# Attention with two heads in halves of the array's rows, four chunks of 112 tokens a unit

## The chip, the core and the metric

The kernel runs on one core of a Trainium2 chip. The metric is the device time of one execution in microseconds (us), taken as the median of several. The engines that matter here are TensorE (PE in the profile, with its weight loads shown apart as PEld), VectorE (DVE), ScalarE (ACT), GpSimd (POOL), and SyncE (SP), which issues most of the DMAs. Matmuls accumulate in PSUM, which has eight banks of 2 KB a partition; a bank holds 512 float32 columns. A matmul uses as many rows of the 128x128 array as its contraction has elements, and as many columns as its weights have.

## The reference

Attention over 8 batches, 12 heads, 448 tokens and a head size of 64, with RMS-normed queries and keys; then a top-1 mixture of experts over the 3584 tokens of 768 features.

```python
q_n, k_n = (rmsnorm(q, g_q), rmsnorm(k, g_k))
scores = scale * np.matmul(q_n, k_n.transpose(0, 1, 3, 2))
scores = scores - np.max(scores, axis=-1, keepdims=True)
attn = np.exp(scores)
attn = attn / (np.sum(attn, axis=-1, keepdims=True) + 1e-09)
attn_out = np.matmul(attn, v)
x = attn_out.transpose(0, 2, 1, 3).reshape(3584, 768)
logits = x @ w_gate + modality_bias[modality_id]
e_idx = np.argmax(logits, axis=1)           # one of 8 experts
gate_w = softmax(logits)[np.arange(3584), e_idx]
for e in range(8):
    mask = e_idx == e
    h = np.maximum(x[mask] @ w1[e], 0.0)    # 768 to 1024
    out[mask] = gate_w[mask, None] * (h @ w2[e])
```

## The kernel before, in words

**Order.** The program is a list of instructions for each engine, in an order that is written out by hand. The attention is a loop over steps n; a table PLAN says at which step each piece of a unit is issued, relative to the unit's own steps. Small operations of the routing wait in a list, and a function pump releases a few of them at each step. Waits between engines follow from the tiles: an instruction that writes a tile waits for the instructions that still read it. Such a dependence goes by the tile, and one allocated twice from a pool of two buffers gives two tiles that don't depend on each other.

**Units and steps.** A unit is one batch and one pair of heads, so there are 48. In the kernel before it has 2 x 448 = 896 keys, cut into seven tiles of 128; tile 3 straddles the two heads. Each unit has seven steps.

**Preparing q and k.** `norm` scales q and k by their root mean squares on POOL; the squares are taken on ACT and summed on DVE (`sumsq`). `tr` (L750) transposes four blocks of 112 tokens of both heads on PE into one PSUM bank, 64 features of head 0 above 64 of head 1. The result is split in two parts of lower precision so that products come out accurate: ACT copies a high part (`a0`), DVE subtracts it to get the low part. Then ACT makes two more copies of half the partitions each (`a1`, `a2`, with a 64x64 copy each for q), and SP issues moves by DMA (`move`, L763), so that the operands stand twice, or stacked high above low. In a unit there are eight such moves of 112 KB.

**Scores.** `sa` (L827, and L822 for tile 3) computes a first product, queries by keys, of 128 rows, one matmul a step into a bank of the pool ps_a (two buffers). DVE takes the maxima of its rows (TENSOR_REDUCE, 128x448). `mt` (L838) transposes the unit's maxima, and a DMA puts them as a 65th row under the low part of q. `st` (L855) computes the scores again, transposed and accurate, with two matmuls a step (128 rows, then 65 rows with the maxima subtracted; four for tile 3) into a bank of ps_s (two buffers). ACT takes the exponential into p.

**Behind the scores.** `av` (L894) multiplies p with v, head 0 into the upper and head 1 into the lower half of the array's columns. These are full float32, and the profile counts two records for each matmul. The eight matmuls of a unit are issued in three visits, in its steps 1, 4 and 6, one unit later. `csum` adds the tiles of p on POOL and DVE for the sums of rows; `sums` and `gates` (L909, L916) compute sums and routing logits; `xt` (L951) turns the output to token rows.

**MoE.** The second part of the program takes the tokens in slots of 256, 14 of them fixed. A slot transposes its tokens in three groups (`xtr`, L464 on; the name of its PSUM tile is px, from ps_a), splits each result in high (ACT) and low (DVE), and runs `mm1` (ph, L485, from ps_s, 18 matmuls for each half of four tiles, evacuated by ACT and DVE) and `mm2` (py, L515). The three transpose groups for the next slot stand within the `mm2` of the present one, at places 9, 11 and 13.

## Time and profile before

| what | value |
|---|---|
| runs | 1123.1, 1125.59, 1126.49 us; median 1125.59 |
| profiled execution | 1126.66 us; its span 1124.8 us |
| first scores matmul (st) starts | 42.1 us |
| last st, then first ph of the MoE | 576.0, then 577.8 us |
| PE busy share of the span | 95% |
| DVE, ACT, POOL busy shares | 77%, 73%, 59% |

The span is cut at 42.1, 577.8 and 662 us: until 42.1 the first unit is prepared, until 577.8 the steps of the attention run, until 662 the first MoE work overlaps the last of the routing, and from there on the MoE runs steadily. A view by windows gives for each stretch the busy time of each engine, with the number of instructions in brackets. A timeline gives one instruction, or several alike, per row: the start, the time, the engine, the line, and the result with its operands. Successive matmuls overlap in their records, so their spacing is read from the starts and not from the durations.

### The profile page before, as it was taken

The page shows a single profiled execution, that of the slowest core. Times are in us where ns is not written, and L with a number is a line of the kernel's source. Part 1 is how long each engine was busy: PE and PEld are TensorE (multiplying, and loading weights), DVE is VectorE, ACT ScalarE, POOL GpSimd, SP SyncE. Part 2 cuts the span into 40 slices and gives each one's busy share as a digit, 9 for nine tenths or more (in the row PEclk, how much of TensorE's full clock was granted, in tenths as well). Part 3 has the DMA queues.
Part 4 walks back from the last instruction along what each step waited for, and adds up shares of the span by engine and source line. Part 5 has one row for each costly group of instructions (what it writes and reads, how often), then busy time and mean ns, then how long its engine had stood idle before and what let it go on. Part 6 is the DMA issues. An engine that isn't in the chain of part 4 may idle for free.

```text
span 1124.8 us, 19920 instructions
## 1 busy us (share of the span) xinstructions
PE 1074.1 (95%) x6678; PEld 837.5 (74%) x6678; DVE 863.4 (77%) x1604; ACT 821.5 (73%) x1545; POOL 659.5 (59%) x658
## 2 busy tenths in 40 slices
PE   7899999999999999998999999999999999999993
PEld 6655555555555555554569989999999999999991
DVE  4677788888889877899699977667777677776770
ACT  5678888878778787876677577667876678766870
POOL 4477677778777688787865474354234432445440
PEclk7999999999999999999999999999999999999997
DMA  6656676677666777665833202111170111111360
GB/s 169 150 137 163 147 180 167 158 172 172 154 169 147 172 161 182 146 145 111 239 124 92 48 29 66 29 58 57 43 267 29 57 58 43 33 40 57 100 207 8
DMA packets 127969, 131.79 MB, mean 117 GB/s; under 512 B 68891, under 2 KB 122607, under 8 KB 126320
## 3 DMA queue, kind: packets, MB, share of 16 engines
q1 hardware_dynamic: 110212, 88.58, 33.5%
q0 software_dynamic: 17616, 41.80, 11.8%
q8 instruction: 57, 0.93, 0.4%
q14 instruction: 56, 0.46, 0.1%
q10 hardware_dynamic: 28, 0.01, 0.0%
HBM read 148.74 MB, written 22.38 MB: 152 GB/s over the span
## 4 chain that ended last, share of the span: by engine, by line
PE 75%; DVE 11%; DMA 7%; ACT 2%; issue 2%; POOL 1%; SPq 1%; ACTq 0%; DVEq 0%; POOLq 0%
PE ph L485 18%; PE py L515 16%; PE av L894 12%; PE st L855 12%; PE sa L827 5%; DMA lt<-l_d,tb_li 4%; PE tr L750 3%; DVE w1w L52 2%; DVE at_hlw L52 2%; PE xt L951 2%; PE sm L909 2%; PE px L468 2%; DMA w1w<-xw 1%; DVE xw L52 1%; DVE w2lw L52 1%
## 5 line engine op out<-in xcount | busy, mean ns | idle before, releaser
L485 PE MATMUL ph<-xw,w1w 128*128 128x256 f32 x2016 | 247.6, 285 | 3.0 <-DVE hlw L52 2.3
L485 PEld LDWEIGHTS ph<-xw,w1w 128*128 128x128 f32 x2016 | 245.3, 193 | 5.0 <-DVE hlw L52 2.5
L52 DVE TENSOR_REDUCE at_hlw<-sa 128x1 f32<-128x448 f32 x336 | 206.6, 617 | 44.4 <-PE sa L827 25.5
L52 DVE TENSOR_TENSOR w1w<-r,w1w 128x256 fp32r<-128x256 f32 x360 | 221.4, 672 | 13.3 <-ACT w1w L52 13.3
L52 ACT CAST w1w<-r 128x256 fp32r<-128x256 f32 x360 | 225.3, 732 | 0.5 <-DVE tb_t L53 0.4
L855 PE MATMUL st<-w1w 128*128 128x448 f32 (+1 forms) x480 | 175.5, 415 | 1.6 <-ACT r2w L52 1.6
L52 ACT ACTIVATE r2w<-st 128x448 f32<-128x448 f32 x168 | 90.9, 543 | 49.7 <-PE st L855 42.0
L52 ACT ACTIVATE hhw<-ph 128x512 fp32r<-128x512 f32 x56 | 33.5, 598 | 124.5 <-PE ph L485 124.5
L827 PE MATMUL sa<-w1w 128*128 128x448 f32 (+1 forms) x288 | 110.9, 386 | 14.1 <-DVE at_hlw L52 7.1
L855 PEld LDWEIGHTS st<-w1w 128*128 128x128 f32 (+1 forms) x480 | 84.8, 190 | 44.2 <-ACT r2w L52 21.8
L52 POOL TENSOR_TENSOR r2w<-r2w 128x448 f32<-128x448 f32 (+1 forms) x72 | 82.9, 1151 | 57.6 <-DVE r2w L52 18.5
L515 PE MATMUL py<-w2lw,hhw 128*128 128x384 f32 x448 | 114.0, 335 | 0.0
L52 ACT ACTIVATE at_w2lw<-st 128x448 f32<-128x448 f32 x168 | 90.9, 543 | 23.3 <-PE st L855 17.3
L52 ACT CAST w1w<-xw 64x448 fp32r<-64x448 f32 x188 | 105.3, 561 | 2.0
L855 PE MATMUL st<-w1w,w2ha 65*128 65x448 f32 x288 | 100.7, 370 | 1.8 <-DMA w1w<-xw 1.7
L52 POOL TENSOR_TENSOR xrw<-r,at_hlw 112x512 f32<-112x512 f32 x94 | 96.9, 1050 | 1.0 <-PE tr L750 0.7
L52 POOL DMA_INDIRECT out_dram<-yw,lb_oi x22 | 25.3, 1152 | 122.2 <-ACT yw L52 112.3
L515 PEld LDWEIGHTS py<-w2lw,hhw 128*128 128x128 f32 x448 | 80.9, 188 | 0.0
L52 DVE SCALAR_TENSOR_TENSOR hlw<-ph,hhw 128x512 fp32r<-128x512 f32 x56 | 38.7, 690 | 53.4 <-ACT hhw L52 53.4
L827 PEld LDWEIGHTS sa<-w1w 128*128 128x128 f32 (+1 forms) x288 | 55.3, 192 | 27.4 <-DVE at_hlw L52 13.0
L52 POOL TENSOR_TENSOR r2w<-r2w,at_w2lw 64x448 f32<-64x448 f32 (+1 forms) x48 | 55.3, 1152 | 30.3 <-DVE r2w L52 11.3
L52 POOL DMA_INDIRECT xrw<-x_d,lb_x2i x24 | 30.3, 1261 | 67.0 <-DMA xrw<-x_d,lt 63.4
(296 smaller groups left out, 2284.9 us busy)
## 6 DMA issues: line engine op xcount, KB each, us to landing
w1w<-xw SPq DMA_DIRECT2D x312, 112.0 KB
r<-in_q_dram SPq DMA_DIRECT2D x48, 224.0 KB
r<-in_k_dram SPq DMA_DIRECT2D x48, 224.0 KB
...
```

The costliest lines, as they stand in the source:

```text
L52: return fn(*a, **kw)
L468: PE.transpose(ps[:, i, 128 * t : 128 * t + 128], xr[t][:, 2 * g + i], idn)
L485: PE.matmul(ps[:, i], lhsT=lt_, rhs=rt_[:, c], start=n == 0, stop=n == 17)
L515: PE.matmul(ps[n][:, :384], lhsT=lt_[:, j, 128 * t : 128 * t + 128], rhs=rt_[:, 384 * n : 384 * n + 384], start=j == 0 and m == 0, stop=j ...
L750: PE.transpose(sp[:, c], src[:, c], idn[:CP, :CP])
L827: PE.matmul(ps[:, :S], lhsT=t["qq"][r, h, a : a + 128], rhs=t["kk"][h][r], start=True, stop=True)
L855: PE.matmul(ps[:, :S], lhsT=l, rhs=t["qq"][:, h] if first else t["ql"][:, h], start=first and (j != 3 or h == 0), stop=not first and (j != ...
L894: PE.matmul(t["av"][64 * h : 64 * h + 64, :S], lhsT=vv[r, u % 3, j], rhs=t["p"][r, j], start=c == 0, stop=c == 3)
L909: PE.matmul(R[g][32 * i : 32 * i + 32, :S], lhsT=sel[:, m], rhs=T[u + i // 2]["cs"][:, i % 2], start=m == 0, stop=False, tile_position=(0, ...
L951: PE.transpose(ps[:CP, 128 * c : 128 * c + 128], T[u]["xt"][:, c * CP : (c + 1) * CP], idn)
```

## The change

The chunk of keys and queries becomes 112 tokens of both heads (CP), and a unit four steps. Operands stay as the transposes leave them, with head 0 in partitions 0 to 63 (LO) and head 1 in 64 to 127 (HI). A new function `both_heads` issues for each pair of operands two matmuls of 64 rows, one on each half of the array's rows, into the two banks of one PSUM tile. The first product has one such pair a chunk, the accurate scores have four: high by high, low by high, high by low, and a pair that subtracts the maxima (ones in one row of each half, times a row `mr` of maxima). So a unit has 40 such matmuls in place of 23.

The two pools have one buffer of two banks each now. Their tiles, `pa` and `pb`, are allocated once and used for the whole program; the MoE's px, ph and the like take the two banks of pa or pb in turn through `bank`. One maximum and one exponential cover a chunk of both heads. The copies a1 and a2 and all eight moves a unit are gone; the maxima go through two small DMAs, and v is loaded by one DMA a unit in place of four. The low parts and high copies are issued in the step of their transposes, behind the exponential and the maximum. The four av pieces have a step each, behind the transposes of the step. PLAN has new numbers throughout, for steps of which there are four a unit; the loop starts at step -14 of these, before at -22 of the others.

```diff
-NJ = 7
+NJ = 4
-PLAN = {'rtj': 6, ..., 'av': (1, 1, 4, 6), ..., 'sa': 14, 'mt': 6, 'tk': 21, 'tq': 18, ..., 'start': -22, ...}
+PLAN = {'rtj': 1, ..., 'av': (0, 1, 2, 3), ..., 'sa': 7, 'mt': 3, 'tk': 9, 'tq': 10, ..., 'start': -14, ...}
...
-    ps_a = ctx.enter_context(tc.tile_pool(name="ps_a", bufs=2, space=PSUM))
-    ps_s = ctx.enter_context(tc.tile_pool(name="ps_s", bufs=2, space=PSUM))
+    ps_a = ctx.enter_context(tc.tile_pool(name="ps_a", bufs=1, space=PSUM))
+    ps_s = ctx.enter_context(tc.tile_pool(name="ps_s", bufs=1, space=PSUM))
...
+    pa = ps_a.tile([128, 2, 512], F32, tag="a", name="pa")
+    pb = ps_s.tile([128, 2, 512], F32, tag="s", name="pb")
+    turns = [0, 0]
+
+    def bank(w):
+        turns[w] ^= 1
+        return (pa, pb)[w][:, turns[w]]
...
     def xtr(s, xr, g):
-        ps = ps_a.tile([128, 2, TB], F32, tag="a", name=f"px{s}_{g}")
+        ps = bank(0).rearrange("p (i t) -> p i t", i=2)
...
     def mm1_open(s, jj):
-        return ps_s.tile([128, 2, TB], F32, tag="s", name=f"ph{s}_{jj}")
+        return bank(1).rearrange("p (i t) -> p i t", i=2)
...
+            SY.dma_start(t["v"][:CP, u % 3].rearrange("p h c d -> p h (c d)"),
+                         v[b, h0 : h0 + 2].rearrange("h (p c) d -> p h (c d)", p=CP))
...
-            h_, l_ = hi_b[u % 2][g], lo_b[g]
+            h_, l_ = t[nm] = qk_b[u % 4][2 * g : 2 * g + 2]
...
+        def both_heads(ps, c, *operands):
+            for n, (l, r) in enumerate(operands):
+                for h, rows in enumerate((LO, HI)):
+                    PE.matmul(ps[:CP, h, :S], lhsT=l[rows] if l is mone else l[rows, CP * c : CP * c + CP],
+                              rhs=r[rows],
+                              start=n == 0, stop=n == len(operands) - 1)
...
+            both_heads(pa, c, (t["q"][0], t["k"][0]))
 
             def dve():
-                V.tensor_reduce(out=t["mx"][:, j : j + 1], in_=ps[:, :S], op=ALU.max,
-                                axis=AX.X, negate=True)
+                V.tensor_reduce(out=t["mx"][:, :, c], in_=pa[:CP, :, :S], op=ALU.max, axis=AX.X, negate=True)
...
+                for h in range(2):
+                    SY.dma_start(t["mr"][64 * h : 64 * h + 1].bitcast(F32),
+                                 ms[NCH * h : NCH * h + NCH].bitcast(F32))
...
+            (qh, ql), (kh, kl) = t["q"], t["k"]
+            both_heads(pb, c, (kh, qh), (kl, qh), (kh, ql), (mone, t["mr"]))
 
             def act():
-                A.activation(out=t["p"][:, j], in_=ps[:, :S], func=AF.Exp)
+                A.activation(out=t["p"][:CP, c], in_=pb[:CP, :, :S], func=AF.Exp)
...
+            for h in range(2):
+                o = (c2_b if c < NCH - 1 else t["cs"])[:CP, h]
+                (V if c == 1 and h in CSV else G).tensor_tensor(
+                    out=o, in0=p[:CP, 0, h] if c == 1 else c2_b[:CP, h], in1=p[:CP, c, h], op=ALU.add)
...
-                j, r = (3, (LO, HI)[h]) if c == 3 else (4 * h + c, slice(0, 128))
-                PE.matmul(t["av"][64 * h : 64 * h + 64, :S], lhsT=vv[r, u % 3, j],
-                          rhs=t["p"][r, j], start=c == 0, stop=c == 3)
+                PE.matmul(t["av"][64 * h : 64 * h + 64, :S], lhsT=vv[:CP, u % 3, h, c],
+                          rhs=t["p"][:CP, c, h], start=c == 0, stop=c == NCH - 1)
```

**PE in the attention.** The first steps of a unit in the middle of the program stand on PE like this before (a row is an instruction with its line, result, operands and shape, and the semaphores that it waits for, each named after the engine or the DMA queue that raises it):

```order
L855 MATMUL st_0_2884<-w1w 128x448 [waits Activation_49]
L855 MATMUL st_0_2884<-w1w 128x448 [waits DMAHW7_49,DMAHW6_49,DMAHW2_49]
L827 MATMUL sa_0_2887<-w1w 128x448 [waits DMAHW3_49,DMAHW0_49,DVE_49]
L750 MATMUL tr_1_2889<-idn,xrw 128x112 [waits PE_49,Pool_49]
L750 MATMUL tr_1_2889<-idn,xrw 128x112 x3
L855 MATMUL st_1_2902<-w1w 128x448 [waits Activation_49]
L855 MATMUL st_1_2902<-w1w 128x448
L827 MATMUL sa_1_2905<-w1w 128x448 [waits DVE_49]
L894 MATMUL av_2907<-r2w 64x448 [waits Activation_49]
L894 MATMUL av_2907<-r2w 64x448 x3
L838 MATMUL mt_2912<-idn,at_hlw 7x128
```

And so after (both_heads is L750 now, tr L728, av L809):

```order
L750 MATMUL pa<-w1w 112x448 [waits DVE_49]
L750 MATMUL pa<-w1w 112x448
L750 MATMUL pb<-w1w 112x448 [waits Activation_49]
L750 MATMUL pb<-w1w 112x448 x7
L728 MATMUL tr_0_4428<-idn,xrw 128x112 [waits PE_49,Pool_49]
L728 MATMUL tr_0_4428<-idn,xrw 128x112 x3
L809 MATMUL av_4383<-at_w2lw 64x448 x2
L750 MATMUL pa<-w1w 112x448 [waits DVE_49]
L750 MATMUL pa<-w1w 112x448
```

A step now issues its two sa matmuls first, which wait for DVE, then eight st matmuls, which wait for ACT, then a transpose and two av matmuls; before, st stood first and alternated with single sa matmuls, and av came in fours.

**DVE in the attention.** Before, where the maxima of two steps of a unit stand (the rows with sa), with the low part of k (xw<-tr) and a sum of squares (at_hlw<-xrw):

```order
L52 SCALAR_TENSOR_TENSOR r2w<-at_w2lw,half 128x448 [waits Activation_49,Pool_49]
L52 TENSOR_REDUCE at_hlw<-xrw 112x8 [waits Activation_49]
L52 TENSOR_REDUCE at_hlw<-sa_0_3263 128x1 [waits PE_49]
L52 SCALAR_TENSOR_TENSOR xw<-tr_1_3265,gs,xw 128x448 [waits DMAHW6_49,DMAHW7_49,DVE_49,Activation_49]
L52 TENSOR_REDUCE at_hlw<-xrw 112x8
L52 TENSOR_REDUCE at_hlw<-sa_1_3281 128x1 [waits PE_49]
L52 TENSOR_REDUCE at_hlw<-sa_2_3303 128x1 [waits PE_49]
```

After, the maxima read pa, and low parts (w1w<-tr) stand behind the maximum of their own step:

```order
L52 TENSOR_TENSOR w1w<-tr_0_3057,w1w 128x448 [waits Activation_49]
L52 TENSOR_TENSOR r2w<-r2w 112x448 [waits Pool_49]
L52 TENSOR_REDUCE at_hlw<-pa 112x2 [waits PE_49]
L52 SCALAR_TENSOR_TENSOR w1w<-tr_1_3082,gs,w1w 128x448 [waits Activation_49]
L52 TENSOR_REDUCE at_hlw<-xrw 112x8 [waits Activation_49]
L52 TENSOR_REDUCE at_hlw<-pa 112x2 [waits PE_49]
L52 TENSOR_TENSOR at_w2hb<-xt_3109,rs_144 112x4x128 [waits PE_49]
L52 TENSOR_REDUCE at_hlw<-xrw 112x8 [waits Activation_49]
L52 TENSOR_REDUCE at_hlw<-pa 112x2 [waits PE_49]
```

The sum of squares and the low part of k stand between two maxima in both; there are four maxima a unit where there were seven, and a low part no longer waits for DMA queues.

**PE in the MoE.** The three groups of transposes of one slot before, where "..." leaves out the py matmuls between:

```order
L468 MATMUL px_0_9067<-idn,xrw 128x128 [waits DMASW6_49]
L468 MATMUL px_0_9067<-idn,xrw 128x128 [waits DMASW0_49]
L468 MATMUL px_0_9067<-idn,xrw 128x128 x2
...
L468 MATMUL px_1_9094<-idn,xrw 128x128 x4
...
L468 MATMUL px_2_9129<-idn,xrw 128x128 [waits DVE_49]
L468 MATMUL px_2_9129<-idn,xrw 128x128 x3
```

And the same groups after:

```order
L464 MATMUL pa<-idn,xrw 128x128 [waits DMASW2_49]
L464 MATMUL pa<-idn,xrw 128x128 [waits DMASW4_49]
L464 MATMUL pa<-idn,xrw 128x128 x2
...
L464 MATMUL pa<-idn,xrw 128x128 [waits DVE_49]
L464 MATMUL pa<-idn,xrw 128x128 x3
...
L464 MATMUL pa<-idn,xrw 128x128 [waits DVE_49]
L464 MATMUL pa<-idn,xrw 128x128 x3
```

Before, the third group waits for DVE (by the value of the semaphore, for the low part of the first group, whose buffer it takes). After, the second group waits for DVE too, for the low part of the first, and the third for that of the second, as all three are in one tile. For ph the same holds: the second half of a tile's 36 matmuls now stands behind the evacuation of the tile before it.

More of the change, by code (lines that the diff above doesn't have):

```diff
@@ L114 @@
     btmp = cp.tile([CP, B * NCH, NE], F32, name="btmp")
-    half = cp.tile([128, 2], F32, name="half")
-    V.memset(half, 0.0)
-    V.memset(half[0:64, 0:1], 1.0)
-    V.memset(half[64:128, 1:2], 1.0)
     lnb = cp.tile([128, 2], F32, name="lnb")
@@ L400 @@
     ra_b, rz_b = SS + 48 * 4, SS + 48 * 5
-    mx_b = [view(sw, SS + 288 + 8 * i, 128, NJ) for i in range(2)]
+    mx_b = [view(sw, SS + 288 + 8 * i, CP, 2, NCH) for i in range(2)]
     rs_b = [cp.tile([CP, NCH, 4, 2], F32, name=f"rs{i}") for i in range(2)]
@@ L562, in half_slot @@
         for jj in range(4):
-            ps = ps_s.tile([128, 512], F32, tag="s", name=f"pw{s}_{jj}")
+            ps = bank(1)
             n = 0
@@ L584, in small_slot @@
         tk = slice(0, SMALL)
-        px = ps_a.tile([128, 512], F32, tag="a", name=f"qx{s}")
+        px = bank(0)
         for c in range(6):
@@ L683, in sumsq @@
             sq = sq_b[i]
-            if (u, i) in PLAN["pa"]:
-                x = T[u][nm].rearrange("p h c d -> p (h c) d")
-                for n in range(2 * NCH):
-                    A.activation(out=sq[:, n], in_=x[:, n], func=AF.Square,
-                                 accum_out=t["ss"][:, i, 8 * j + n : 8 * j + n + 1])
-                return lambda: None
             A.activation(
@@ L695, in reduce @@
             def reduce():
-                if (u, i) in PLAN["ps"]:
-                    o = t["ss"][:, i, 8 * j : 8 * j + 8].unsqueeze(2)
-                    w = D // 2
-                    while w:
-                        G.tensor_tensor(out=sq[:, :, 0:w] if w > 1 else o, in0=sq[:, :, 0:w],
-                                        in1=sq[:, :, w : 2 * w], op=ALU.add)
-                        w //= 2
-                    return
                 V.tensor_reduce(
@@ L846, in mt, with st @@
             return act
-        def st(u, j):
+        def st(u, c):
             t = T[u]
-            if j == 0:
+            if c == 0:
                 t["p"] = p_b[u % 2]
-            ps = ps_s.tile([128, 512], F32, tag="s", name=f"st{u}_{j}")
-            for first in (True, False):
-                for h, l in columns(t["kkf" if first else "khf"], j):
-                    PE.matmul(ps[:, :S], lhsT=l, rhs=t["qq"][:, h] if first else t["ql"][:, h],
-                              start=first and (j != 3 or h == 0), stop=not first and (j != 3 or h == 1))
+            (qh, ql), (kh, kl) = t["q"], t["k"]
+            both_heads(pb, c, (kh, qh), (kl, qh), (kh, ql), (mone, t["mr"]))
@@ L908, in sums @@
             for i in range(4):
-                PE.matmul(R[g][32 * i : 32 * i + 32, :S], lhsT=sel[:, m],
-                          rhs=T[u + i // 2]["cs"][:, i % 2], start=m == 0, stop=False,
+                PE.matmul(R[g][32 * i : 32 * i + 32, :S], lhsT=sel[:CP, m],
+                          rhs=T[u + i // 2]["cs"][:CP, i % 2], start=m == 0, stop=False,
                           tile_position=(0, 32 * i))
@@ L1107 @@
         P = PLAN
-        CSV, CSJ, CSD, CSE = (P[x] for x in ("csv", "csj", "csd", "cse"))
+        CSV = P["csv"]
         def at(where, n, fn):
@@ L1144 @@
         for u in range(NU):
-            for j in range(NJ):
-                jj = (0, 1, 2, 4, 5, 6, 3)[j] if u < P["early"] else j
-                put(when("sa", u) + j * (P["sastep"] if u == 0 else 1), "sa", u, jj)
+            for c in range(NCH):
+                put(when("sa", u) + c, "sa", u, c)
             put(when("mt", u), "mt", u)
@@ L1209 @@
                 at(pre["V"], n + 1, xt(*a))
-            if puts and n >= puts[0][0] and n - lastput[0] >= 3:
+            for u, c in todo.get("av", ()):
+                av(u, c)
+                if c == NCH - 1:
+                    at(pre["A"], n + 1, lambda u=u: avcopy(u))
+            for a in todo.get("sums", ()):
+                sums(*a)
+            for a in todo.get("gates", ()):
+                at(pre["A"], n + 1, gates(*a))
+            if puts and n >= puts[0][0] and n - lastput[0] >= 2:
                 lastput[0] = n
@@ L1228 @@
             pump(P["rush"][2] if state["rush"] else P["pmp0"] if n < P["ramp"] else 0, j)
[L1229 to L1233 removed]
+            if 0 <= i < NU and j > 0:
+                at(fin, n + 1, lambda u=i, c=j: csum(u, c))
             run(fin, n)
```

194 lines of the change are left out of this document (49 added, 145 removed).

## The prediction

> **What bounds the kernel now.** I read the busy shares first, then the chain of waits, then the stages apart, since an average over attention and MoE tells of neither.
>
> ```profile
> PE 1074.1 (95%) x6678; PEld 837.5 (74%) x6678; DVE 863.4 (77%) x1604; ACT 821.5 (73%) x1545; POOL 659.5 (59%) x658
> PE ph L485 18%; PE py L515 16%; PE av L894 12%; PE st L855 12%; PE sa L827 5%; DMA lt<-l_d,tb_li 4%; PE tr L750 3%; DVE w1w L52 2%; DVE at_hlw L52 2%; PE xt L951 2%; PE sm L909 2%; PE px L468 2%; DMA w1w<-xw 1%; DVE xw L52 1%; DVE w2lw L52
> ```
>
> PE is busy for 95% of the span, and the chain that ended last lies on PE for the most part: the MoE's products (ph, py) and, of the attention, av, st and sa. By stages:
>
> ```profile
> 0.00:42.10 42.10, 34.73 (x186) 30.53 (x187) 23.57 (x55) 23.07 (x48) 15.52 (x38) 0.80 0.65 161
> 42.10:577.80 535.70, 520.28 (x2788) 299.05 (x2786) 442.39 (x867) 428.66 (x933) 409.96 (x431) 1.00 0.68 159
> 662.00:1125.00 463.00, 438.96 (x3149) 433.12 (x3148) 320.85 (x501) 311.37 (x473) 184.96 (x158) 0.98 0.22 70
> ```
>
> From 42.1 to 577.8 us PE works 520.28 of 535.70 us. That is 10.84 us of work for each of 48 units and 0.32 of waiting, 11.16 in all. DVE is next with 442.39 (9.2 a unit), ACT has 428.66 (8.9), and the DMA engines 0.68 of their time. So only what shortens PE's own row of work shortens the attention, and a wait laid on PE lengthens it. In the MoE PE has 438.96 of 463 us. One piece of PE's timeline prices the work:
>
> ```profile
> 350.01 0.37 PE L827 MATMUL sa<-w1w 128*128 128x448 f32 x1
> 350.22 0.57 PE L855 MATMUL st<-w1w 128*128 128x448 f32 x2
> 350.63 0.37 PE L827 MATMUL sa<-w1w 128*128 128x448 f32 x1
> 350.93 0.97 PE L894 MATMUL av<-r2w 64*64 64x448 f32 x4
> 351.83 0.47 PE L855 MATMUL st<-w1w 128*128 128x448 f32 x1
> 352.14 0.37 PE L855 MATMUL st<-w1w,w2ha 65*128 65x448 f32 x1
> ...
> 352.88 0.55 PE L750 MATMUL tr<-idn,xrw 112*128 112x112 f32 x4
> 353.20 0.45 PE L855 MATMUL st<-w1w 128*128 128x448 f32 x1
> ...
> 353.99 1.73 PE L894 MATMUL av<-at_w2lw 128*64 128x448 f32 x8
> 355.64 0.28 PE L838 MATMUL mt<-idn,at_hlw 128*7 128x128 f32 x1
> ...
> 356.48 0.57 PE L909 MATMUL sm<-at_w2hb,sel 128*32 128x448 f32 x2
> 356.49 0.57 PE L909 MATMUL sm<-at_hhw,sel 128*32 128x448 f32 x2
> 356.88 0.55 PE L909 MATMUL sm<-at_w2hb,sel 128*32 128x448 f32 x2
> 356.89 0.55 PE L909 MATMUL sm<-at_hhw,sel 128*32 128x448 f32 x2
> 357.37 0.68 PE L855 MATMUL st<-w1w 128*128 128x448 f32 x2
> ```
>
> Starts follow each other by 0.205 us in a run of full matmuls of 448 columns (350.01, 350.22, then 350.63 after two). From the last sa to av pass 0.30, so changing from the whole array to column halves costs about 0.10. One av piece, two heads' matmuls in four records, takes 0.90 until the next st (350.93 to 351.83), and two pieces 1.65 (353.99 to 355.64): 0.75 a piece and 0.15 on leaving. The first st after such a change is followed by the next after 0.31 instead of 0.205 (351.83 to 352.14), 0.10 more. The sums, four matmuls of 32 columns in eight records, take 0.89 until the next st (356.48 to 357.37), no more than the two of av, and start 0.01 apart: in this kernel tiles of columns run side by side. Nothing in the trace shows two tiles of rows doing so.
>
> **PE's work after the change.** A unit had 7 sa and 16 st matmuls, 23 x 0.205 = 4.7 us. It gets 40 of 64 rows, in 20 pairs. If a pair shares the array as the column tiles do, it takes one stream of 448 columns: 20 x 0.205 = 4.1, a gain of 0.62. The bounds are this and 40 x 0.205 = 8.2 (no sharing, a rival below); I take the sharing, by the nearest rows, those of the sums. The av pieces are as many, but in four visits for three: one more entry and exit, 0.10 + 0.15 + 0.10 = +0.35. The change from halves of rows to the whole array (tr, mt) or to columns (av) and back is not in the trace. At least it costs nothing beyond the 0.35. At most each of the four returns in a unit costs 0.10 more, as a return to the whole array does now: 0 to +0.4, of which I take +0.2, the middle. Together 10.84 - 0.62 + 0.35 + 0.2 = 10.77 a unit, between 10.57 and 10.97.
>
> The Trainium skill has a rule on each side of this. "TensorE: Matmul & The Clock Gate", Measured speedup vs the span model, gives 3.07 for four tiles of 32 rows, near the time of one matmul with some 4 ns for each further tile; this case's rows show the like for columns only. "TensorEngine Tiling (Array Packing)", Key Properties, says "Changing tiling mode (not just tile) drains the TensorE", which speaks against a step that goes from row halves to the whole array to column halves; the 0.10 at each change above agrees. By that rule the upper end, +0.4, would be the value and the forecast some 10 us higher.
>
> **The waits that single tiles bring.** This is where I see most of the risk. Before, sa and st each had two buffers. Now sa of the next step waits for the maximum of this one, and st for the exponential.
>
> ```profile
> L827 PE MATMUL sa<-w1w 128*128 128x448 f32 x276 | 104.0, 377 | 11.0 <-DVE at_hlw L52 5.9 <-DMA w1w<-xw 4.2 <-issue 0.7
> L52 DVE TENSOR_REDUCE at_hlw<-sa 128x1 f32<-128x448 f32 x63 | 38.8, 616 | 5.3 <-PE sa L822 3.5 <-PE sa L827 1.8
> L52 DVE TENSOR_REDUCE at_hlw<-xrw 112x8 f32<-112x512 f32 x18 | 12.1, 674 | 0.0
> L52 DVE TENSOR_TENSOR xw<-tr,xw 128x448 fp32r<-128x448 f32 x9 | 5.6, 620 | 1.6 <-ACT xw L52 1.6
> 305.29 0.61 DVE L52 TENSOR_REDUCE at_hlw<-sa 128x1 f32<-128x448 f32 x1
> 305.82 0.69 DVE L52 TENSOR_TENSOR yw<-xt,rs 112x512 f32<-112x512 f32 x1
> L52 ACT ACTIVATE r2w<-st 128x448 f32<-128x448 f32 x168 | 90.9, 543 | 49.7 <-PE st L855 42.0
> L52 ACT ACTIVATE hhw<-ph 128x512 fp32r<-128x512 f32 x56 | 33.5, 598 | 124.5 <-PE ph L485 124.5
> L52 ACT CAST w1w<-xw 64x448 fp32r<-64x448 f32 x35 | 19.6, 561 | 0.4
> L52 ACT CAST xw<-xw 64x64 fp32r<-64x64 f32 x10 | 2.4, 239 | 0.0
> ```
>
> Even with two buffers sa waits 5.9 us in all for DVE. After a maximum of 448 columns the next operation of DVE follows in 0.53 us (305.29 to 305.82); 64 columns more, as the sums of squares have, add 0.058 by their means (674 to 616 ns), so 896 columns are estimated at 0.53 + 7 x 0.058 = 0.94 to twice 0.53 = 1.06, say 1.0. Four of these, 4.0 us, for seven of 0.53, 3.7: DVE gains nothing, and stays at 9.2 to 9.5 us a unit. The exponential of 896 columns comes to about 0.93 (543 ns for 448 columns, 598 for 512: 55 ns for 64): 3.7 a unit for 7 x 0.543 = 3.8. ACT drops the copies, four of 0.561 and two of 0.24 a unit, 2.7 us, and SP the eight moves. None of these is on PE's path now: PE's waits for moved operands at sa are 4.2 us for the whole stage, 0.09 a unit, and these do go.
>
> Between the end of one sa pair and the next PE has 0.82 of st, 0.3 of tr (352.88 to 353.20), and 0.9 of av, about 2.0 us. A maximum of 1.0 fits if DVE begins it within 1.0. Between the end of one st and the next stand tr, av and sa, about 1.4 to 1.5, and an exponential of 0.93 fits if ACT begins it within about 0.5. On ACT a high copy (0.53) or a square (0.63) may be under way at that moment, on DVE a sum of squares (0.67) and a low part (0.62) follow a maximum in most steps: 1.0 + 0.62 + 0.67 = 2.3 within a step of 2.8. Alone these fit, barely. But DVE has lumps, the recips and the routing's small operations, in about 9.3 of 11.2 us, and with one buffer nothing runs ahead to absorb them. So I expect waits of 0.2 to 0.8 us a unit, less where DVE catches up while PE waits. I take 0.45, for 0.32 now. What queues behind a late sa is the whole step: eight st, then av, and for these the next exponential.
>
> Stage: 10.77 + 0.45 = 11.22 for 11.16, +0.06 x 48 = **+3 us**; the ends are 10.57 + 0.2 and 10.97 + 0.8, 10.77 to 11.77, or -19 to +29.
>
> **The start.**
>
> ```profile
> 15.64 0.47 PE L827 MATMUL sa<-w1w 64*128 64x448 f32 x1 [1.94 <-ACT w1w L52]
> L855 PEld LDWEIGHTS st<-w1w x480: 186/190/338, 42.1 to 576.0; 128*128 128x128 f32 x128, 65*128 65x128 f32 x32
> ```
>
> The first sa stands at 15.64 and the first st at 42.1: 26.5 us for fourteen short steps, in which the moves and PE's fillers keep the steps apart. After the change seven steps lie between them. DVE is the engine with the most to do there: seven maxima (7.0), eight sums of squares at their spacing of 0.60 (4.8), three low parts (1.7) and one norm of about 0.6, 14.1 us from some 15 us on, and 1.5 to 2 of waits. So the first st comes near 31: **-11 us**; between -7, if the waits are as many as now, and -13, with none.
>
> **The MoE.** Its code is the same, but a group of transposes waits for the evacuation of the group before it.
>
> ```profile
> 732.52 0.68 PE L468 MATMUL px<-idn,xrw 128*128 128x128 f32 x4
> 733.38 0.68 DVE L52 TENSOR_TENSOR xw<-px,xw 128x512 fp32r<-128x512 f32 x1
> 735.15 0.68 PE L468 MATMUL px<-idn,xrw 128*128 128x128 f32 x4
> 736.22 0.67 DVE L52 TENSOR_TENSOR xw<-px,xw 128x512 fp32r<-128x512 f32 x1
> ...
> 622.47 0.81 PE L468 MATMUL px<-idn,xrw 128*128 128x128 f32 x4 [1.51 <-DVE xw L52]
> ...
> 702.22 17.43 PE L485 MATMUL ph<-xw,w1w 128*128 128x256 f32 x144
> 707.36 0.69 DVE L52 SCALAR_TENSOR_TENSOR hlw<-ph,hhw 128x512 fp32r<-128x512 f32 x1 [0.86 <-ACT hhw L52]
> ```
>
> In this slot the second px stands at 732.52. The low part of the first is taken by DVE at 733.38 for 0.68, so until 734.06 the second must wait now: +1.54 us. Shifted by that, the third would stand at 736.7, where DVE's low part of the second (736.22 + 0.67 = 736.89) ends 0.2 later. PE stands still meanwhile, as py is queued behind: 1.75 a slot. That such a wait does stop PE shows at 622.47, where it cost 1.51 already. Twelve slots repeat the steady pattern, and the first gives some 3 more: 12 x 1.75 + 3 = **+24 us**. At least it is nothing, if ACT and DVE, less busy than PE here (311.37 and 320.85 of 463), take up the delay and reach the low parts sooner; at most some 30. For ph the wait is covered: 17.43 us for four tiles are 4.36 each, so the second half of tile 1 begins at 702.22 + 1.5 x 4.36 = 708.8, and the low part of tile 0 is done at 707.36 + 0.69 = 708.05. If that cover of 0.7 were gone, each 0.1 beyond it would cost 14 x 3 x 0.1 = 4 us.
>
> **Sum.** The profiled execution took 1126.66, 1.07 above the median of the runs. 1126.66 + 3 - 11 + 24 = 1142.7, or about **1142 us** against the median. Its own range by the bounds runs from 1115 to 1170.
>
> **Rivals.**
> *(a) Faster.* Row pairs go with free changes (10.57), ACT and DVE, rid of their waits for moves, run ahead so that a unit waits 0.2 us, and in the MoE they reach the low parts sooner, so that only +8 is left: 48 x (10.77 - 11.16) = -19, -11, +8, or 1104 us. For it: ACT loses 2.7 us a unit, and DVE no longer waits for DMA queues. Against it: DVE's total doesn't fall, and the px waits hang on one slot's order. Chance 0.28.
> *(b) Halves of rows take turns.* Then 40 x 0.205 = 8.2 us a unit for 4.1, +4.1 x 48 = +197. The waits for DVE and ACT vanish behind the longer work (-0.45 x 48 = -22): 1142 + 197 - 22 = 1317. A spacing of the pairs above 4.7 / 20 = 0.235 us already loses the gain of 0.62. For it: no row here shows row tiles together. Against it: column tiles do. Chance 0.08.
> *(c) Weight loads don't hide.*
>
> ```profile
> 350.43 0.19 PEld L827 LDWEIGHTS sa<-w1w 128*128 128x128 f32 x1
> ```
>
> A load takes 0.19 us, and here it runs while a matmul uses the whole array. If with halves it had to wait for its half to come free, each pair would need its 0.19 beside its 0.205: 20 x 0.19 = 3.8 a unit, less 0.45 of hidden waits, +161, 1303. The Trainium skill, "TensorE: Matmul & The Clock Gate", What overlaps and what doesn't, has loads overlap a matmul only in other groups of rows; the row above shows otherwise. Chance 0.04.
>
> The forecast keeps 0.60. Against no change, 0.3% is what a measurement here can tell: 1122 to 1129. Case (a) lies below it but for a trace; of the forecast's own range some 0.07 lies below 1122 and 0.11 within. That gives faster 0.28 + 0.6 x 0.07 = 0.32, same 0.08, slower 0.60. The range, 1098 to 1172, leaves out (b) and (c) with 0.12 and tails of some 0.07.
>
> **What would show it.** In the changed profile a pair of halves should start within some 0.01 us and pairs follow by about 0.205; a spacing of 0.41 is (b), one of 0.4 with PE's loads in the gaps (c). The groups of PE should show waits at both_heads for DVE's maxima and ACT's exponentials of 10 to 38 us in the attention, the first st near 31, and the px rows waits for xw of 1 to 2 us in each slot. If px shows none, or the attention's steps last under 2.7 us each, the forecast is wrong on the low side, toward (a).

## The result, and the profile after

The changed kernel takes 1263.16 us in the median of 4 runs (1260.52 to 1270.33), the kernel before 1125.19: 1.124 times as long, with a 95% interval of 1.119 to 1.129. The forecast was slower, but 1142 us, and the range ended at 1172. The profiled execution took 1270.33 us, the slowest of the four, so its stages differ by some 144 us from those before, and the medians by 138.

By stages, from the first instructions named in each trace (the forecast's terms in the last column):

| stage | before | after | difference | forecast |
|---|---|---|---|---|
| until the first st | 42.1 | 33.6 | -8.5 | -11 |
| attention, to the first ph of the MoE | 535.7 | 583.1 | +47.4 | +3 |
| first ph to the end | 547.0 | 651.9 | +104.9 | +24 |

The windows of the profile after, with the columns as before (busy time of PE, PEld, DVE, ACT, POOL, then PE's granted clock and the share of the DMA engines):

```profile
33.60:616.70 583.10, 538.72 (x3598) 267.86 (x3598) 452.05 (x739) 308.15 (x518) 407.79 (x426) 0.97 0.27 74
616.70:1268.60 651.90, 538.53 (x3706) 512.98 (x3706) 397.69 (x676) 372.47 (x567) 219.03 (x189) 0.97 0.20 61
```

What PE waited for, in total, times and longest, first in the attention, then in the MoE:

```profile
PE pa L750 <- DVE at_hlw L52: 31.3, 40, 2.4
PE xt L866 <- DVE w1w L52: 8.3, 3, 4.5
...
PE pb L481 <- DVE hlw L52: 63.4, 41, 5.7
PE pa L464 <- DVE xw L52: 21.6, 15, 2.4
```

In the MoE PE stands 63.4 us for hlw, the low part of ph, and 21.6 for xw, the low part of px. Before, the first was 2.3 us and the second 2.0. A piece of the timeline shows the first kind. ph in these rows is pb, px is pa:

```profile
805.81 6.62 PE L481 MATMUL pb<-xw,w1w 128*128 128x256 f32 x54
812.54 0.60 ACT L52 ACTIVATE hhw<-pb 128x512 fp32r<-128x512 f32 x1 [4.24 <-issue]
813.16 0.69 DVE L52 SCALAR_TENSOR_TENSOR hlw<-pb,hhw 128x512 fp32r<-128x512 f32 x1 [3.07 <-ACT hhw L52]
813.91 4.57 PE L481 MATMUL pb<-xw,w1w 128*128 128x256 f32 x36 [1.47 <-DVE hlw L52]
...
842.83 0.80 PE L464 MATMUL pa<-idn,xrw 128*128 128x128 f32 x4 [1.50 <-DVE xw L52]
```

A tile of ph has 36 matmuls. Here 54 run first, the tile and the first half of the next, and only then ACT begins the evacuation of the first tile, at 812.54. Before, ACT and DVE did that while PE ran the next tile: DVE's low part stood at 707.36, 5.1 us after the first ph of its slot; now it stands 7.35 after it. In program order the evacuation stands behind the first half of the next tile. As both tiles are banks of one PSUM tile now, it waits for those matmuls, and the second half of the next tile (36 matmuls from 813.91) waits for it. PE stands still for 1.47 us, three times a slot. At 842.83 the second group of px waits 1.50 us for the low part of the first, as the order had shown.

In the attention a step looks like this where nothing is late:

```profile
503.67 0.46 PE L750 MATMUL pa<-w1w 64*112 64x448 f32 x2
503.96 0.96 PE L750 MATMUL pb<-w1w 64*112 64x448 f32 x8
504.86 0.60 PE L728 MATMUL tr<-idn,xrw 112*128 112x112 f32 x4
505.39 0.97 PE L809 MATMUL av<-at_w2lw,r2w 112*64 112x448 f32 x4
506.29 0.46 PE L750 MATMUL pa<-w1w 64*112 64x448 f32 x2
507.49 0.65 PE L866 MATMUL xt<-idn,at_hlw 128*112 128x128 f32 x4
508.06 0.97 PE L809 MATMUL av<-r2w 112*64 112x448 f32 x4
...
510.17 0.26 PE L768 MATMUL mt<-idn,at_hlw 112*8 112x112 f32 x1
510.35 0.97 PE L809 MATMUL av<-r2w 112*64 112x448 f32 x4
```

The pair of sa takes 0.29 us, four pairs of st 0.90, both with the change to the next group. So two halves do share the array. But tr takes 0.53 to the next group, where it was 0.32 (352.88 to 353.20), mt 0.18 where the next group began 0.04 behind it (355.64 to 355.68), and xt 0.57 where it was 0.40. The rows of xt before:

```profile
360.50 0.65 PE L951 MATMUL xt<-idn,at_hlw 128*112 128x128 f32 x4
360.90 0.45 PE L855 MATMUL st<-w1w 128*128 128x448 f32 x1
```

Where PE is late it is for DVE, and some of this comes in lumps. The worst place but one:

```profile
240.42 2.25 POOL L52 TENSOR_TENSOR r2w<-r2w,at_w2lw 112x448 f32<-112x448 f32 x2
241.32 4.56 DVE L53 TENSOR_TENSOR oh<-i_e,ei 112x32 f32<-112x32 f32 x1
242.62 1.04 POOL L52 TENSOR_TENSOR xrw<-r,at_hlw 112x512 f32<-112x512 f32 x1
243.62 2.20 POOL L52 TENSOR_TENSOR at_w2hb<-r2w,at_w2lw 112x448 f32<-112x448 f32 x2
245.80 0.67 DVE L52 SCALAR_TENSOR_TENSOR w1w<-tr,gs,w1w 128x448 fp32r<-128x448 f32 x1
246.53 0.72 PE L866 MATMUL xt<-idn,at_hlw 128*112 128x128 f32 x4 [3.42 <-DVE w1w L52]
```

DVE's comparison of 32 columns (oh), which took 0.49 us on average in the kernel before, lasts 4.56, and ends as GpSimd's run of additions and norms ends. PE's transposes then wait 3.42 us. The Trainium skill, "SBUF — State Buffer", Who interferes with whom, says that a DVE instruction with two inputs in SBUF contends with GpSimd's reads; these rows agree. PE pays for such a stop a second time: in the 15 us behind this wait its granted clock is 0.55, and a step takes 4.77 us (254.30 to 259.07 in the trace) where one of the same kind takes 2.62 above:

```profile
246.50:261.70 15.20, 14.86 (x61) 7.56 (x63) 9.40 (x21) 3.00 (x5) 5.41 (x5) 0.55 0.17 46
```

### The profile page after: what moved, and what is told of

It is laid out like the page before. It is cut to its first block, busy times and chain, and to the rows that moved or that the text cites. A ratio compares the mean times of both kernels' runs of the same rounds, so it can differ in the third digit from the quotient of the medians.

```text
span 1268.6 us, 19967 instructions
## 1 busy us (share of the span) xinstructions
PE 1105.4 (87%) x7502; PEld 805.9 (64%) x7502; DVE 872.3 (69%) x1457; ACT 694.9 (55%) x1111; POOL 638.9 (50%) x649
## 3 DMA queue, kind: packets, MB, share of 16 engines
q1 hardware_dynamic: 45056, 44.52, 13.2%
## 4 chain that ended last, share of the span: by engine, by line
PE 40%; DVE 19%; issue 17%; ACT 11%; POOL 5%; DMA 5%; another core or an unknown queue 1%; SPq 0%; ACTq 0%; POOLq 0%; DVEq 0%
PE pb L750 9%; PE av L809 8%; PE pb L481 7%; DVE at_hlw L52 6%; ACT w1w L52 5%; PE py L511 4%; PE pa L750 4%; DVE w1w L52 4%; DMA lt<-l_d,tb_li 4%; PE tr L728 2%; PE sm L824 2%; POOL r2w L52 1%; ACT w2ha L52 1%; DVE w2lw L52 1%; ACT at_w2lw L52 1%
## 5 line engine op out<-in xcount | busy, mean ns | idle before, releaser
L481 PE MATMUL pb<-xw,w1w 128*128 128x256 f32 x2016 | 261.1, 289 | 71.5 <-DVE hlw L52 63.4
L481 PEld LDWEIGHTS pb<-xw,w1w 128*128 128x128 f32 x2016 | 251.1, 195 | 81.7 <-DVE hlw L52 72.4
L52 DVE TENSOR_REDUCE at_hlw<-pa 112x2 f32<-112x896 f32 x192 | 208.2, 1084 | 47.8 <-PE pa L750 47.5
L52 DVE TENSOR_TENSOR w1w<-r,w1w 128x256 fp32r<-128x256 f32 x360 | 219.8, 668 | 17.2 <-ACT w1w L52 17.2
L750 PE MATMUL pb<-w1w 64*112 64x448 f32 x1536 | 191.9, 368 | 2.8 <-ACT at_w2lw L52 1.7
L52 ACT ACTIVATE r2w<-pb 112x896 f32<-112x896 f32 x96 | 88.0, 917 | 132.5 <-PE pb L750 126.6
L750 PEld LDWEIGHTS pb<-w1w 64*112 64x112 f32 x1536 | 137.9, 176 | 23.8 <-ACT r2w L52 3.7
L52 ACT ACTIVATE at_w2lw<-pb 112x896 f32<-112x896 f32 x96 | 88.1, 917 | 114.3 <-PE pb L750 98.7
L750 PEld LDWEIGHTS pa<-w1w 64*112 64x112 f32 x384 | 33.9, 173 | 168.1 <-DVE at_hlw L52 109.0
L52 POOL TENSOR_TENSOR r2w<-r2w 112x448 f32<-112x448 f32 x72 | 83.0, 1154 | 79.0 <-ACT w1w L52 37.9
L750 PE MATMUL pa<-w1w 64*112 64x448 f32 x384 | 90.2, 466 | 35.1 <-DVE at_hlw L52 34.5
L52 DVE TENSOR_REDUCE at_hlw<-xrw 112x8 f32<-112x512 f32 x96 | 64.7, 678 | 4.4 <-ACT xrw L52 3.9
```

Source lines behind the costliest of these rows:

```text
L52: return fn(*a, **kw)
L481: PE.matmul(ps[:, i], lhsT=lt_, rhs=rt_[:, c], start=n == 0, stop=n == 17)
L750: PE.matmul(ps[:CP, h, :S], lhsT=l[rows] if l is mone else l[rows, CP * c : CP * c + CP], rhs=r[rows], start=n == 0, stop=n == len(operand ...
```

## The experiments

The chips differ by up to one per cent, so each ratio is to the kernel before on the same chip, with its 95% interval where there is one. The changed kernel itself stands at 1.124.

### Which part of the MoE's loss is the shared tile

**e1, own banks in the MoE**

```diff
...
+        if two[w] is None:
+            own[w].__exit__(None, None, None)
+            two[w] = ctx.enter_context(tc.tile_pool(name="ab"[w] + "2", bufs=2, space=PSUM, ...))
-        turns[w] ^= 1
-        return (pa, pb)[w][:, turns[w]]
+        return two[w].tile([128, 512], F32, tag="as"[w], name="p" + "xh"[w])[:, :]
```

> The changed kernel with one thing put back: at the start of the MoE the two shared tiles pa and pb are released and two pools of two single-bank tiles each take their place, so that px and ph go by bank again; the attention is untouched. Theory 'one tile': an evacuation of ph stands in program order behind the first half of the next tile, and as both lie in one tile it waits for those matmuls, and the second half then waits for the evacuation; the transposes px wait for the group before. Then PE's waits for hlw (63.4 us) and xw (21.6 us) in the MoE fall to the 4 us of the kernel before, with up to 10 us more from restarts and clock: 1263 - 81 to - 95 = 1168 to 1182 us. Rival 'aftermath': the MoE is slower because of what the attention leaves behind (late routing, late weights, a halved clock); then the tiles matter little and the time stays above 1240 us.

**e2, the same for ph alone**

> As e1, but only ph gets two single-bank tiles; the transposes px stay in pa. Theory 'one tile': the ph part alone is 61 to 70 us, 1193 to 1202 us, and px's waits for xw stay near 21 us. By the prediction, which held ph's wait for covered, it would gain nothing and the time would stay at 1263 us.

**e3, the kernel before with one tile in the MoE**

```diff
...
-        ps = ps_a.tile([128, 2, TB], F32, tag="a", name=f"px{s}_{g}")
+        ps = bank(0).rearrange("p (i t) -> p i t", i=2)
...
-        return ps_s.tile([128, 2, TB], F32, tag="s", name=f"ph{s}_{jj}")
+        return bank(1).rearrange("p (i t) -> p i t", i=2)
...
```

> The reverse: the kernel before, attention untouched, with px and ph in the two banks of one tile each for the MoE alone. Theory 'one tile': it loses what e1 wins, 81 to 105 us, 1206 to 1230 us, with waits of PE of about 63 us for hlw and 21 us for xw. Rival 'aftermath': no attention of the new kind went before it, so it stays at 1125 to 1140 us.

e1 takes 1155.08 us, a ratio of 1.0195 (1.0158 to 1.0232); e2 1188.39, 1.049 (1.042 to 1.056); e3 1230.63, 1.086 (1.080 to 1.093). The groups of ph and px (busy, mean, idle before and its releaser), of the kernel before, of the changed one, of e1 and of e3:

```profile
L485 PE MATMUL ph<-xw,w1w 128*128 128x256 f32 x2016 | 247.6, 285 | 3.0 <-DVE hlw L52 2.3 <-DVE xw L52 0.6
L468 PE MATMUL px<-idn,xrw 128*128 128x128 f32 x168 | 28.9, 295 | 2.3 <-DVE xw L52 2.0 <-DVE rtc L52 0.3
```

```profile
L481 PE MATMUL pb<-xw,w1w 128*128 128x256 f32 x2016 | 261.1, 289 | 71.5 <-DVE hlw L52 63.4 <-issue 5.0 <-DVE xw L52 1.6
L464 PE MATMUL pa<-idn,xrw 128*128 128x128 f32 x168 | 32.1, 313 | 21.6 <-DVE xw L52 21.6
```

```profile
L485 PE MATMUL ph<-xw,w1w 128*128 128x256 f32 x2016 | 246.3, 283 | 4.1 <-DVE xw L52 3.0 <-DVE hlw L52 1.0
L468 PE MATMUL px<-idn,xrw 128*128 128x128 f32 x172 | 29.6, 295 | 2.8 <-DVE xw L52 2.4 <-DVE rtc L52 0.3
```

```profile
L498 PE MATMUL ph<-xw,w1w 128*128 128x256 f32 x2016 | 261.0, 289 | 64.4 <-DVE hlw L52 62.4 <-issue 2.0
L481 PE MATMUL px<-idn,xrw 128*128 128x128 f32 x176 | 33.7, 314 | 22.0 <-DVE xw L52 22.0
```

With its own banks the MoE is as fast as before: from the first to the last ph it takes 496.7 us in both (577.8 to 1074.5, and 605.2 to 1101.9), 599.0 in the changed kernel. Of the 102 us some 84 are idle time of PE (90.1 us for 6.5 before), and in the other 19 or so PE is busy for longer with the same matmuls (508.9 us for 490.2), in restarts and at a clock of 0.99 for 1.00. By the medians e1 gains 0.104 of 1134 us on the changed kernel, 118, more than the 81 to 95 expected of it, and e2 0.075, 85, for 61 to 70. Restarts and clock had been put at 10 us at most, and in e1 the MoE also begins 11 us earlier (605.2 for 616.7), though its attention is the same program: there the waits differ from one execution to the next. In e3 an attention that was not touched is followed by the same waits, 62.4 and 22.0 us. So the loss is the tile's and "aftermath" is wrong. ph is some 75 us of it by the rows (63.4 of idle time for 2.3, 261.1 of busy time for 247.6) and 85 by e2; px is some 23 (21.6 for 2.0, and 32.1 for 28.9), and 33 by the difference of e1 and e2.

### Do halves of rows run together

**e4, all of head 0, then all of head 1**

```diff
-            for n, (l, r) in enumerate(operands):
-                for h, rows in enumerate((LO, HI)):
+            for h, rows in enumerate((LO, HI)):
+                for n, (l, r) in enumerate(operands):
```

> The kernel of e1 with the matmuls of both_heads in another order: all operand pairs of head 0 in the lower half of the rows, then all of head 1 in the upper half. If two halves run together only when neighbours in the order use different halves, st goes from about 0.91 us a step to 7 or 8 times 0.205 = 1.44 to 1.64 us: +0.5 to +0.7 for 192 steps, +100 to +140 us on e1, less some 30 us of waits that the longer steps hide, so +70 to +140. If the halves never run together (the rival of the prediction), the order makes no difference and the time is that of e1.

**e5, both on one half**

```diff
-                for h, rows in enumerate((LO, HI)):
+                for h, rows in enumerate((LO, LO)):
```

> The kernel of e1 with both matmuls of each pair on the lower half of the rows (head 1's scores are left out: head 0's are computed twice, so its output is no attention of head 1). It tells why e4's order cost so little. Theory 'streams': each half is a stream of its own, which starts its next matmul without regard to the order across halves, and one matmul of 64 rows and 448 columns takes 0.205 us of its half. Then ten matmuls in one half take 2.05 us a step for 1.2 now, +0.9 for 192 steps less what waits it hides, +120 to +165 us on e1's 1155: 1275 to 1320. Rival 'short matmuls': a matmul of 64 rows takes 0.1 us by itself, and halves don't share at all; then the time stays within 10 us of e1.

e4 takes 1169.4 us in its one run, 14 more than e1 and far from the +70 to +140. By its expectation alone that would speak for halves that never run together; e5, which leaves out the scores of head 1, tells. It takes 1390.86 us in its one run. The st of one step and the group behind it, first e4, then e5:

```profile
507.19 1.07 PE L754 MATMUL pb<-w1w 64*112 64x448 f32 x8
508.19 0.65 PE L870 MATMUL xt<-idn,at_hlw 128*112 128x128 f32 x4
```

```profile
303.93 1.77 PE L754 MATMUL pb<-w1w 64*112 64x448 f32 x8
305.63 0.60 PE L732 MATMUL tr<-idn,xrw 112*128 112x112 f32 x4
```

Eight matmuls on one half take 1.70 us, 0.21 each, so "short matmuls" is wrong. The four of one half and then four of the other take 1.00 us, where a start in program order would need at least 3 x 0.21 + 4 x 0.21 = 1.47. So the matmuls of the second half start before all of the first half's are through. The Trainium skill, "TensorE: Matmul & The Clock Gate", What overlaps and what doesn't, calls matmuls "strict FIFO, no reordering"; between halves of rows these rows show otherwise. e5 lost 236 us on e1, more than the 165 at most: PE's granted clock was 0.917 over the span, for 0.982 in e1, so clock was lost too. The profile page's clock row of e5 (40 slices of 34.7 us) has it in two stretches:

```profile
PEclk9555699999999999999557999999999999999997
```

Both lie in the attention, whose last st stands at 842 us. What set them off no run here shows.

### What makes PE wait in the attention

The next runs start from e1, with the MoE out of the way; e9 to e11 also have e6's later low parts.

**e6, low parts a step later**

```diff
-                at(post, n, d_)
+                at(post, n + 1, d_)
```

> The kernel of e1 with DVE's subtraction for the low parts issued one step later, behind the next maximum. In the changed kernel DVE sits idle 45.0 + 16.6 us before these, waiting for ACT's high copy, with the next maximum behind it. Theory 'order on DVE': with that gone PE's waits for maxima (31.3 us) at least halve, and the halved clock that follows some of the waits shrinks too: -16 to -30, 1125 to 1139 us. Rival 'load of DVE': its work comes in lumps beside 85% use, and the order matters little: 1150 to 1158.

**e7, half of the maximum** (`in_=pa[:CP, :, : S // 2]`)

> The kernel of e1 with each maximum taken over half of the keys alone (the subtracted value is then no longer the row's maximum; the other half of the maximum's work is left out). DVE has 0.5 us less in each of 192 steps. Theory 'load of DVE': PE's waits for maxima go nearly all, with the halved clock behind them: -27 to -42, 1113 to 1128 us. Theory 'lumps' (DVE's operations that stand still while GpSimd works, 4.4 and 5.7 us in two places): only 5 to 15 us go, 1140 to 1150.

**e8, av in two visits** (`'av': (1, 1, 3, 3)`)

> The kernel of e1 with the four av pieces of a unit issued in two steps, two at a time, in place of one in each step: two changes fewer between halves of rows and halves of columns. At 0.15 to 0.2 us a change each way, as av's 0.90 against 0.75 us a piece shows, 2 x 0.17 x 48 = 14 to 19 us go if PE sets the pace: 1136 to 1141. If the waits for maxima set it, the gain turns into waits and the time stays above 1150.

e7 leaves out half of each maximum. e6 takes 1149.55 us, 1.017 (1.010 to 1.024); e7 1130.68, 1.0005 (0.997 to 1.004); e8 1187.54, 1.049 (1.042 to 1.057). PE's waits in e1, e6 and e7:

```profile
PE pa L754 <- DVE at_hlw L52: 32.2, 39, 2.2
```

```profile
PE pa L754 <- DVE at_hlw L52: 19.6, 23, 3.0
PE sp L847 <- DVE w1w L52: 7.3, 9, 3.4
```

```profile
PE pa L754 <- DVE at_hlw L52: 16.8, 22, 1.7
```

e6 lowers the waits for maxima from 32.2 to 19.6 us, but 7.3 come back where sp waits for a bank that a later low part still reads; its gain, 0.003 of the time, lies within the intervals. e7 wins 0.019, between the ranges of its two theories: taking 0.5 us a step from DVE halves the waits. Its first ph stands at 577.8 us as in the kernel before, but its first st at 32.2 in place of 42.1, so the attention is still 10 us longer. The row of it:

```profile
32.20:577.80 545.60, 525.51 (x3598) 263.03 (x3598) 363.34 (x738) 308.79 (x518) 408.32 (x426) 1.00 0.29 79
```

PE runs the same instructions there as in the changed kernel, at a clock of 1.00 for 0.97, and is busy 525.51 us for 538.72. e8 went the other way, and shows why:

```profile
306.24 0.46 PE L754 MATMUL pa<-w1w 64*112 64x448 f32 x2
306.53 0.98 PE L754 MATMUL pb<-w1w 64*112 64x448 f32 x8
...
308.02 0.46 PE L754 MATMUL pa<-w1w 64*112 64x448 f32 x2
308.58 1.08 PE L754 MATMUL pb<-w1w 64*112 64x448 f32 x8
...
311.78 0.46 PE L754 MATMUL pa<-w1w 64*112 64x448 f32 x2
```

The step without av lasts 1.78 us (306.24 to 308.02), the next 3.76. Together that is 5.54, where two even steps of this kind took 5.24 (2 x 2.62, 503.67 to 506.29 in the changed kernel). Behind the short step st starts 0.56 after sa in place of 0.29, since ACT's exponential leaves pb at 308.54. With one buffer each step costs what its slowest engine needs, and PE cannot make up in a long step what it lost in a short one.

**e9 to e11, DVE's work given to others.** Sums of squares go to ACT as eight squares with a running sum (e9 for q, e10 for q and k), and in e11 also DVE's addition of row sums to GpSimd (`'csv': ()`):

```diff
+                        A.activation(out=sq[:, n], in_=x[:, n], func=AF.Square,
+                                     accum_out=t["ss"][:, i, 8 * j + n : 8 * j + n + 1])
```

> The kernel of e6 with the sums of squares of q (from unit 6 on) added up on ACT by eight squares of 64 columns with a running sum, four in one step and four in the next, in place of one square on ACT and one sum of 0.6 us on DVE. e7 took 2.0 us a unit from DVE and won 24 us, so the 'load of DVE' gives 12 us a us: 0.6 a unit is -7 on e6's 1149.5, 1140 to 1145 us. If ACT's longer row (8 x 0.24 for 0.63, +1.3 us a unit beside 6.4 now) makes the exponentials late, it is 1150 or more, with PE's waits for ACT's exponentials above the 1.2 us of e1.

> As e9 for q and k: 1.2 us a unit less on DVE, 2.5 more on ACT. 'Load of DVE': -14 on e6, 1132 to 1139 us. If ACT becomes the bound: 1150 or more.

> As e10, and the one addition of row sums that DVE did (0.8 us a unit) on GpSimd, which has 8.6 us a unit and gets 1.15 more. 'Load of DVE': 2.0 us a unit less on DVE, as in e7: -24 on e6, 1122 to 1130 us. Rival: DVE's operations on SBUF stand still while GpSimd works, so GpSimd's longer row gives back what DVE saves, and GpSimd's norms may come late: 1135 or more.

All three lost: 1162.86 (1.029; 1.022 to 1.036), 1172.97 (1.036; 1.028 to 1.045) and 1164.28 us (1.031; 1.024 to 1.038). The groups on ACT in e10, and PE's waits there:

```profile
L52 ACT ACTIVATE xrw<-r 112x64 f32<-112x64 f32 x655 | 158.1, 251 | 0.0
L52 ACT ACTIVATION_READ_ACCUMULATOR xrw<-r 112x1 f32 x656 | 129.0, 197 | 0.0
...
PE sp L858 <- DVE w1w L52: 17.2, 8, 6.2
PE pb L765 <- ACT r2w L52: 6.4, 22, 1.1
```

Each running sum brings an instruction of its own of 0.197 us beside the 0.251 of the square: 16 x 0.448 = 7.2 us a unit for 2 x 0.63, so 5.9 more, where 2.5 had been put down. The waits for maxima fell to 7.3 us, but those for ACT's exponentials rose from 1.4 to 12.6 (6.4 for r2w, 6.2 for the other tile) and those of sp to 17.2. So a price for each microsecond taken from DVE, on which these expectations stood, does not hold when the work goes to ACT: what leaves DVE turns up as a wait at another single buffer. Less work on DVE, with none added elsewhere, is what e7 alone has.

**e12, one tile a head; e13, with low parts later too**

```diff
-            sm = [sa(*a) for a in todo.get("sa", ())]
+            sm = [[sa(*a, 0) for a in todo.get("sa", ())], None]
             ex = st(i, j) if 0 <= i < NU else None
+            sm[1] = [sa(*a, 1) for a in todo.get("sa", ())]
...
-                V.tensor_reduce(out=t["mx"][:, :, c], in_=pa[:CP, :, :S], ...)
+                V.tensor_reduce(out=t["mx"][:, h, c : c + 1], in_=ps[:CP, :S], ...)
```

> The kernel with four single-bank tiles, one for each head: sa of head 0 stands at the start of a step and sa of head 1 behind st; maxima and exponentials are taken for each head (448 columns), the maximum of head 0 ahead of a step's other work on DVE, that of head 1 behind it. PE's and DVE's work is that of e1 (a maximum of 896 columns becomes two of 448, 0.53 us apart). What changes is how long a maximum may be late before PE stands: by the rows of the changed kernel from 1.3 us to some 2. Theory 'coupling' (a tile of one buffer, so that a lump on DVE stops PE in the same step): PE's waits for maxima fall from 32 us to under 12, the halved clock behind them shrinks, 1122 to 1138 us on the chip where e1 took 1155. Rival 'load': the same work on DVE brings the same waits, 1148 to 1160 us.

> As e12, and the low parts one step later as in e6, here right behind the next maximum of head 0, so that DVE does not stand idle for ACT's high copy. 'Coupling': a little more slack, 1115 to 1135 us, and the waits of sp and xt for the low parts that e6 showed (7.3 us) stay under 4, as the low parts come earlier in the step than there. If the order on DVE matters no more once heads are apart, it is within 4 us of e12.

e12 takes 1140.86 us, 1.0093 (1.006 to 1.013); e13 1143.24, 1.012 (1.009 to 1.015). In e12:

```profile
PE sa L746 <- DVE at_hlw L52: 10.2, 16, 1.5
PE xt L865 <- DVE w1w L52: 6.5, 2, 4.7
```

With the same products and maxima the waits for maxima fall from 32.2 to 10.2 us. That is the coupling. The time falls by 0.010 of 1130, 11 us, less than the 17 to 33 expected. In the attention PE's idle time goes down from 38.1 to 17.4 us, but its busy time goes up from 535.1 to 542.4, and DVE's from 445.3 to 464.1: two maxima of 448 columns take 2 x 0.617, one of 896 took 1.084. Why PE is busy for longer stays open. e13 is no better: with heads apart the order of DVE's low parts matters no more. In e12 a lump of GpSimd and DVE stays, in two waits of xt.

**e14 and e15, fewer visits of the whole array.** e14 puts both transposes in one step and xt beside mt (`'tk': 10, 'xt': 1, 'sm': 0`); e15 the transposes only.

> The kernel of e13 with the work of the whole array gathered: both transposes of a unit in one step, xt and the transposed maxima in another, sums a step earlier; the other two steps go from halves of rows straight to halves of columns. Nothing is left out. Theory 'modes': a visit of the whole array between halves of rows and halves of columns costs 0.2 us beyond its own matmuls (tr takes 0.53 to the next group, 0.32 in the kernel before; xt 0.57 for 0.40), two visits fewer a unit are 2 x 0.2 x 48 = 19 us: 1122 to 1128 us on the chip where e13 took 1143, a ratio to the kernel before of 0.993 to 0.999. Rival: steps that are shorter than DVE's and ACT's part (as in e8) turn it into waits: 1140 or more.

> As e13, with only the two transposes of a unit in one step, one visit of the whole array fewer: 'modes' 0.2 x 48 = 10 us, 1131 to 1136 us; the rival 1143 or more.

They take 1152.1, 1.021 (1.017 to 1.025), and 1153.72 us, 1.021 (1.017 to 1.025), both slower than e13. In e14 the two transposes follow each other in one visit, and still take 1.15 us to the next group:

```profile
302.77 1.22 PE L723 MATMUL tr<-idn,xrw 112*128 112x112 f32 x8
303.92 0.97 PE L808 MATMUL av<-r2w,at_w2lw 112*64 112x448 f32 x4
```

The second begins as the evacuation of xt, late on DVE, leaves a bank (302.59 + 0.68 = 303.27, the second's load at 303.38), and in the steps without a visit st is 0.29 us late behind the exponential, as in e8. Over the attention PE's busy time doesn't fall (542.1 us in e14 and 549.4 in e15, 542.3 in e13, at clocks of 1.00, 0.98 and 0.99), and its idle time rises (26.1 and 21.0 for 18.5). So these two runs don't price a change of the array's use by itself. No run that does the whole of the work beat the kernel before; e12 came nearest.

## Why the prediction was wrong

**The step that failed most is "For ph the wait is covered".** It took the evacuation's time, 707.36, from the kernel before and asked only whether the second half of the next tile begins later. It does; but the evacuation itself moved. It stands behind the first half of the next tile in program order, and by the shared tile it waits for it. The order that was quoted shows the wait on PE; the one on ACT, which makes it bite, was not looked at. Instead of 0 it cost some 75 us (61 of idle time and 14 of longer busy time), as e1, e2 and e3 show.

**The waits of px** were put at 24 us; 21.6 of idle time were measured, with 3 of longer busy time. **The start** was put at -11; it was -8.5.

**Halves of rows share the array**: right, and (b) and (c) with their 1300 us are out. Pairs follow each other by 0.2 us, and loads don't stand in the gaps. (a), the faster case, is out too: PE's work a unit is more than before, not less.

**PE's work** was put at 10.77 us a unit, between 10.57 and 10.97, for 10.84 before. At a clock of 1.00 (e7) it is 525.51 / 48 = 10.95: more than before, though less was forecast, but inside the bounds. Counted in the traces from one start to the next over 36 units in the middle, the scores take 4.8 us a unit in e7, av 3.7, and tr, xt and mt together 1.8; before these were 5.7, 3.5 and 1.1. So the scores gained more than the forecast's 0.62: its 4.7 for them left out, for one, the slower first matmul behind tr, mt and the sums (353.20 to 353.49 in place of 0.205). And **"the change from halves of rows to the whole array (tr, mt) or to columns (av) and back"** cost more than the +0.2 that was taken: in steps without a wait tr, xt and mt take 2 x 0.53 + 0.57 + 0.18 = 1.81 for 2 x 0.32 + 0.40 + 0.04 = 1.08. They used the whole array like the scores did, so before they stood beside them at no price; now each lies between halves of rows and halves of columns. That is 0.73 a unit, argued at first from rows at av alone. By luck these errors largely cancel. The rule of the Trainium skill on changing modes ("TensorEngine Tiling (Array Packing)", Key Properties), which would have taken the upper end, came nearest.

**"I take 0.45" for the waits.** PE's idle time is 583.10 - 538.72 = 44.4 us, 0.92 a unit, past the bound of 0.8; 31.3 + 8.3 + 2.8 (exponentials) of it are waits for DVE and ACT. The mechanism was right: e12 shows the coupling. What was missed is the size of the lumps, of which the two largest (4.5 and 3.4 us at xt) come behind a DVE that stands still beside GpSimd.

**The clock was put at nothing.** No term of the sum has it. PE was granted 0.97 in this stage, 1.00 before, and was busy 538.72 us where the same instructions took 525.51 at 1.00 in e7: 13 us. How much of that is clock and how much restarts is not told apart.

So the attention's 47.4 us are 29.0 of idle time (44.4 for 15.4), 13.2 of longer busy time, at the lower clock and in restarts, and 5.2 of work (525.51 for 520.28).

**Sum by terms**: forecast 3 - 11 + 24 = 16 us, measured 47 - 8.5 + 105 = 144. Of the 128 between them some 75 are ph, 44 the attention, 2.5 the start, and some 7 a wait of 5.0 us and other time at the end of the MoE. The forecast's "own range by the bounds", 1115 to 1170, is not the sum of its ends either: -19 - 13 + 0 and +29 - 7 + 30 on 1125.6 give some 1094 to 1178. 1263 lies far outside both.
